# TensorE multiplies a constant in the gaps that its planner leaves

## The chip, the cores and the metric

The kernel runs on one core of a Trainium2 chip. The metric is the device time of one execution in microseconds, as a median of several runs. "PE" is TensorE (the matrix engine), "PEld" its loading of weights, "DVE" VectorE, "ACT" ScalarE, "POOL" GpSimd, "SP" SyncE, which here only issues DMAs. Each engine works through its own instructions strictly in the order in which they were written; engines wait for each other by semaphores.

## The reference: what is computed

One transformer-like block over 2048 tokens of 448 channels: an S4 convolution with adaptive layer norm, then a gated feed-forward layer with another one.

```python
mod = (silu(c) @ w_mod).reshape(6, 448)            # sa, ca, ga, sb, cb, gb
h = layernorm(x) * (1 + ca) + sa
# S4: K[d, l] = Re sum_n C[d,n] * exp(dt*A[d,n] * l) * dt*B[d,n],  448 x 256 complex modes
y = irfft(rfft(pad(h)) * rfft(pad(K))) + h * Dskip
x = x + ga * y
h = layernorm(x) * (1 + cb) + sb
x = x + gb * ((gelu(h @ w_gate) * (h @ w_up)) @ w_down)   # 448 -> 1792 -> 448
```

## The kernel before, in words

The program is written as some 2000 small tasks. Each names the engine (or the choice of engines), a cost in microseconds, a due value, the tasks that it depends on and the buffers that it takes (`Plan.add`, from L148). `Plan.order` (L195) places them one by one: it asks which engine can start soonest, takes for it the ready task with the lowest due value, adds the cost to that engine's clock and sets `t.on` and `t.start`. The due values are corrected by a table of found numbers (`LEAD`, L39). `Plan.run` (L258) then calls each task's function in that order, and the function writes its instructions; so the order of every engine's instructions is the planner's, while the real waits are those of the semaphores that the tile framework adds: an instruction waits for the data that it reads, and the first write to a tile waits until the readers of the buffer before it are done.

The work has three stages.

*Generating the convolution kernel and transforming it (0 to about 375 us).* `prep` (L425) makes the exponents from A, B, C and dt on VectorE and ScalarE and writes them to DRAM as bf16 pieces (`lh_d`), from which `load_lt` fetches them as matmul operands `lt`. `exps` (L583) and `angles` (L621) form exponents and angles on TensorE in PSUM (pool `gen`, two buffers named `pg`), ScalarE takes exp and sin of them, VectorE multiplies (`tx`, `ty`), and `kgen` (L695) sums over the modes with 64 small f32 matmuls into a PSUM tile of the pool `kgp` (buffers `kg`); `ktail` (L720) does a first transform. Meanwhile `mod_row` (L758) makes the rows of `mod`: one DMA of 784 KB (`m.ld`), four f32 matmuls of 448 columns with one column of `c` repeated as weights (`m.mm`, L768), and a copy by ScalarE (`m.ev`, L771). Three rows are needed at the very start; the three DMAs stand on SP's queue behind two 896 KB loads of `x`. `u_norm_a` (L814) normalises `x` and makes the first transform of it (`ua`, L832, two f32 matmuls of 448 columns with 64 rows each), `u_stage_b` and `k_fft` (L959) go on. `m.mm`, `ua` and the transforms share the PSUM pool `fft`, two buffers named `pf`.

*The last part of the transforms and the change-over (about 375 to 425 us).* `t_fft` (L1055) does the last 128 channels; its results go through DRAM into the tile `yi`. `conv_out` (L1227) then makes, for each of the four token groups j of a block, the last transform (`co.mm`, L1246 for the first 320 channels and L1251 for the last 128; for the first block and j below 2 these are two tasks, `co.mme` and `co.mml`, into one PSUM buffer of the pool `pd`), adds `x`, takes the statistics (`co.add`), normalises (`co.n`, L1288 and L1289), transposes the result by an f32 matmul with the identity (`co.t`, L1294 and L1296, into the pool `ps`, six buffers named `pq`) and copies it as f16 high and low parts. This is so for block 0; for the later blocks the transposition is another, in f16 (L1317).

*The feed-forward layer (about 421 us to the end).* `gate_up` (L1338) multiplies with the weights in three f16 products (L1371, L1365), ScalarE takes gelu, VectorE multiplies, and `down_first` and `down` (L1441, L1472) multiply back.

`eps` (L370, L371) is one column of the tile `small`, set to 1e-5 by VectorE as its first instruction; the square roots read it.

## Time and profile before

| | us |
|---|---|
| median of three runs | 823.77 |
| lowest, highest | 823.62, 831.2 |
| the profiled execution, its own time | 825.18 |
| the profiled execution, span from the first to the last instruction | 823.4 |
| TensorE busy in the span | 748.4 |
| VectorE busy | 599.6 |
| ScalarE busy | 470.3 |
| mean granted clock of TensorE | 0.969 |

The profile is of one execution. Its times are counted from the first instruction. A row of the timeline gives the start, the length, the engine, the source line, the operation with the tile that it writes and the one that it reads, a count where neighbouring instructions were merged, and in brackets how long the engine had stood idle before it and what ended that. A row of the waits gives who waited for what, the total in us, how many times, and the longest. A row of a table by stretches gives the busy time of each engine in the stretch (in the order PE, PEld, DVE, ACT, POOL), then the mean granted clock of TensorE (1.00 is full, 0.50 half), the share of the DMA engines' time and the GB/s. The granted clock comes from recorded steps; where none has been recorded yet, the table shows 1.00. Matmul ends are modelled, so that records of matmuls can overlap.

### The profile page before, as it was taken

What the parts mean: (1) busy time and instruction counts of PE and PEld (TensorE: products, weight loads), DVE (VectorE), ACT (ScalarE), POOL (GpSimd) and SP (SyncE); (2) the same over time, 40 slices, a digit from 0 to 9 for tenths busy, and PEclk for the clock granted to TensorE, in tenths of its full rate; (3) what the DMA queues carried; (4) which work ended last, traced back from release to release, by engine and by line L of the source; (5) the groups of instructions that cost most, each with busy time, mean ns of one, the idle gap of its engine ahead of it and who ended that gap; (6) DMA issues with size and microseconds to landing.
All of it is one profiled execution on the core that took longest, in us unless ns stands there. A gap on an engine that the chain in (4) does not pass through costs nothing.

```text
span 823.4 us, 19059 instructions
## 1 busy us (share of the span) xinstructions
PE 748.4 (91%) x8166; PEld 461.2 (56%) x8166; DVE 599.6 (73%) x981; ACT 470.3 (57%) x629; POOL 6.0 (1%) x14
## 2 busy tenths in 40 slices
PE   2786789999799999998589999999999999999997
PEld 1344344444577767778466445444496445864477
DVE  7789998999889989897494783178863686244542
ACT  5598999899968999971244553034442353113320
POOL 0000000000000000000200000000000000000000
PEclk9888799999999999999889999999999999999999
DMA  9552369996858846899669756245315322022101
GB/s 283 148 167 92 105 189 236 285 273 200 236 146 257 233 133 193 253 307 295 189 197 298 267 179 179 75 140 166 117 53 146 135 91 90 34 79 90 45 12 35
DMA packets 92526, 136.83 MB, mean 166 GB/s; under 512 B 21280, under 2 KB 75200, under 8 KB 92442
## 3 DMA queue, kind: packets, MB, share of 16 engines
q1 hardware_dynamic: 89514, 133.75, 53.8%
q10 hardware_dynamic: 2608, 1.61, 0.8%
q8 instruction: 64, 1.05, 0.5%
q0 software_dynamic: 320, 0.26, 0.1%
q14 instruction: 20, 0.16, 0.1%
HBM read 100.48 MB, written 36.01 MB: 166 GB/s over the span
## 4 chain that ended last, share of the span: by engine, by line
PE 67%; ACT 12%; DVE 10%; DMA 6%; issue 3%; SPq 1%; DVEq 0%; ACTq 0%
PE pq L1371 30%; PE pq L1472 9%; PE pd L1441 3%; PE kg L710 3%; ACT fg L643 2%; PE pg L630 2%; PE pf L999 2%; PE pq L1365 2%; PE pf L768 2%; ACT my L617 2%; PE pf L1085 2%; PE pf L895 2%; DVE tx L679 2%; DMA fg<-in_w_mod 2%; PE pd L1472 1%
## 5 line engine op out<-in xcount | busy, mean ns | idle before, releaser
L1371 PE MATMUL pq<-ht,wr 128*128 128x512 f16 (+1 forms) x1200 | 250.0, 367 | 0.0
L1371 PEld LDWEIGHTS <-wr 128*128 128x128 f16 x1200 | 115.4, 98 | 128.6 <-issue 11.0
L1378 ACT ACTIVATE ge<-pq 128x512 f32<-128x512 f32 (+1 forms) x60 | 33.9, 568 | 144.5 <-PE pq L1365 93.9
L1385 DVE TENSOR_TENSOR fq<-ge,pq 128x512 f32<-128x512 f32 (+1 forms) x60 | 38.5, 649 | 72.1 <-PE pq L1371 48.2
L1397 ACT ACTIVATE hh<-fq 128x1024 f16<-128x1024 f32 (+1 forms) x49 | 47.1, 963 | 54.5 <-DVE fq L1385 41.8
L1472 PE MATMUL pq<-d,hh 128*128 128x224 f16 x504 | 73.2, 259 | 0.0
L710 PE MATMUL kg<-ty,tx 128*32 128x64 f32 x3584 | 61.8, 221 | 11.3 <-DVE ty L687 6.4
L679 DVE TENSOR_TENSOR tx<-mx,fg 128x1024 f32<-128x1024 f32 x56 | 68.0, 1220 | 4.0 <-ACT fg L654 2.2
L683 DVE TENSOR_TENSOR ty<-my,fg 128x1024 f32<-128x1024 f32 x56 | 68.2, 1219 | 3.0 <-PE kg L710 2.8
L710 PEld LDWEIGHTS kg<-ty,tx 128*32 128x32 f32 x3584 | 53.0, 110 | 27.6 <-issue 11.2
L1472 PE MATMUL pq<-d,hlo 128*128 128x224 f16 x252 | 65.3, 259 | 0.0
L1400 DVE TENSOR_TENSOR hlo<-fq,hh 128x1024 f16<-128x1024 f32 (+1 forms) x49 | 53.9, 1104 | 5.3 <-ACT hh L1397 5.0
L643 ACT ACTIVATE fg<-pg 128x1024 f32<-128x1024 f32 x56 | 56.6, 1019 | 1.9 <-issue 1.2
L1472 PEld LDWEIGHTS <-hh 128*128 128x128 f16 x588 | 56.7, 98 | 1.1 <-issue 0.4
L617 ACT ACTIVATE my<-pg 128x1024 f32<-128x1024 f32 x56 | 55.3, 1041 | 3.1 <-PE pg L612 2.9
L999 PE MATMUL pf<-q,fc 128*128 128x160 f32 x264 | 42.9, 313 | 0.3 <-DVE q L989 0.3
L630 PEld LDWEIGHTS <-lt 64*128 64x128 bf16 x336 | 20.7, 95 | 37.4 <-issue 20.7
L999 PEld LDWEIGHTS pf<-q,fc 128*128 128x128 f32 x264 | 37.7, 195 | 6.3 <-issue 3.3
L630 PE MATMUL pg<-ea,lt 64*128 64x512 bf16 x168 | 34.9, 389 | 6.2 <-ACT fg L643 4.4
L687 DVE TENSOR_TENSOR ty<-my,fg 128x512 f32<-128x512 f32 x56 | 38.4, 686 | 0.0
L686 DVE SCALAR_TENSOR_TENSOR ty<-my,fg 128x512 f32<-128x512 f32 x56 | 38.4, 685 | 0.0
L735 PE MATMUL kg<-ak,ke 128*64 128x128 f32 x448 | 32.1, 284 | 6.2 <-DVE ke L730 4.4
(172 smaller groups left out, 1196.3 us busy)
## 6 DMA issues: line engine op xcount, KB each, us to landing
wr<-w_d SPq DMA_DIRECT2D x21, 896.0 KB
fc<-in_k_fc SPq DMA_DIRECT2D x20, 576.0 KB
u_d<-so SPq DMA_DIRECT2D x32, 224.0 KB
w<-in_wgu SPq DMA_DIRECT2D x14, 512.0 KB
ui<-u_d SPq DMA_DIRECT2D x10, 672.0 KB
w_d<-wr SPq DMA_DIRECT2D x7, 896.0 KB
fq<-in_wd SPq DMA_DIRECT2D x14, 448.0 KB
us<-uo SPq DMA_DIRECT2D x22, 240.0 KB
```

Source lines behind the costliest of these rows:

```text
L617: A.activation(yb.tile.rearrange("p a b c -> p (a b c)"), pb.tile, AF.Exp)
L630: T.matmul(pa[:, nh * 512:nh * 512 + 512], w, x, start=(k == 0), stop=(k == 2))
L643: A.activation(fb.tile[:, 0].rearrange("p x (n k) -> p n x k", n=2), pb.tile.rearrange("p (n x k) -> p n x k", n=2, x=2), AF.Sin, scale=TW ...
L679: V.tensor_mul(tx.tile, xb.tile[:, xm, None, :].to_broadcast([128, 2, 512]), fb.tile[:, :, 0])
L683: V.tensor_mul(ty.tile[:, 1], yb.tile, fy()[:, 1, :, None, :].to_broadcast([128, 16, 2, 32]))
L710: T.matmul(kg[32 * g:32 * g + 32, 2 * (s % 2) + q, :64], tx[:, r, nh, 4 * q + g], ty[:, r, nh, 4 * q + g], start=(r == 0 and nh == 0), sto ...
L999: T.matmul(pz.tile[:, e % 32 - sl0], fc.tile[:, i, 1 + t], pp.tile[:, t, i], start=(t == 0 and e != 32), stop=(t == 1 and e != 0))
L1371: T.matmul(pb[k].tile[:, ts], wr.tile[:, 4 * lo + t, k, c0:c0 + 128], ht[:, m, ts], start=f % 2 == 0 and i == 0, stop=f % 2 == 1 and i == 9)
L1385: V.tensor_mul(to if half is None else to[:, half:half + 1], *src)
L1397: A.activation(hg.tile[0][:, cb, c], fq.tile[:, c], AF.Copy)
L1400: V.tensor_sub(hg.tile[1][:, cb, c], fq.tile[:, c], hg.tile[0][:, cb, c])
L1472: T.matmul(bank(k)[:, m], x[:, p, q[0], ts], w[:, p, q[1]], start=new and m == 0 and p == 0 and z == 0, skip_group_check=True, stop=i in ( ...
```

## The change

`Plan.run` now notes, for every task that was placed on TensorE, how long the planner's TensorE stands empty in front of it (`t.idle`). A new function `spin` writes matmuls of the constant `eps` with itself into the PSUM tile that the task is about to fill: int((idle - 1.5) / (0.78 w / 448)) of them, w being the columns, if that is positive. The constant is read with stride 0 both as weights (128 x 128) and as the moving operand (128 x w), in f32; each product starts and ends its own accumulation, and the task's own first matmul overwrites the tile. The products are written in front of the task's own matmuls in six kinds of task: `x.mm`, `kgen` (only where it takes a new PSUM tile), `m.mm`, `ua`, `co.mm` with its parts, and `co.t`. The tasks' costs, due values, dependencies and order stay as they are; the planner doesn't count the products.

```diff
     def run(self):
+        free = 0.0
         for t in self.order():
+            if t.on == "PE":
+                t.idle, free = t.start - free, t.start + t.eng["PE"]
             t.fn(t.on) if len(t.eng) > 1 else t.fn()
...
+    def spin(me, dst, w=D):
+        for _ in range(int(max(0.0, me[0].idle - 1.5) / (0.78 * w / D))):
+            T.matmul(dst, eps.to_broadcast([128, 128]), eps.to_broadcast([128, w]), start=True, stop=True)
...
+        me = []
+
         def mm():
             pb.tile = fft.tile([128, D], FT, name="pf")
+            spin(me, pb.tile)
             for t in range(4):
                 T.matmul(pb.tile, c_sb[:, t:t + 1].to_broadcast([DT, 128]), wb.tile[:, t], start=(t == 0), stop=(t == 3))
         t1 = add("m.ld", {"SP": 0.42}, v, ldw, deps[2:], [wb], kb=803)
         t2 = add("m.mm", {"PE": 3.22}, v, mm, [t1, t_si], [pb], [wb])
+        me.append(t2)
...
                 for h in range(2):
                     pbs[h].tile = fft.tile([128, D], FT, name="pf")
+                spin(me, pbs[0].tile)
                 for h in range(2):
                     T.matmul(pbs[h].tile, au[64 * h:64 * h + 64], XT[jb].tile[64 * h:64 * h + 64, j],
                              start=True, stop=True)
             tm = add("ua", {"PE": 0.97}, vv, mm, [tn, c_au], pbs, [XT[jb]])
+            me.append(tm)
...
                     if i == 0:
                         pb.tile = POOLS["pd"].tile([128, D], FT, name="pd")
+                    spin(me, pb.tile[:, c0:c1], c1 - c0)
...
                 pt.tile = POOLS["ps"].tile([128, 4, 128], FT, name="pq")
+                spin(me, pt.tile.rearrange("p k t -> p (k t)")[:, :D])
                 for k in range(3):
                     T.matmul(pt.tile[:, k], xn.tile[:, 128 * k:128 * k + 128], K2["id"], start=True, stop=True)
...
```

In `x.mm` and `kgen` the call is of the same form, on the first 448 columns of the tile `pg` or `kg`.

## The prediction

> **What bounds the kernel now.** I read the page first (busy shares, the 40 slices), then who TensorE waits for, then the stretches where it waits, then the granted clock cut at its own steps. The page:

> ```profile
> span 823.4 us, 19059 instructions
> ...
> PE 748.4 (91%) x8166; PEld 461.2 (56%) x8166; DVE 599.6 (73%) x981; ACT 470.3 (57%) x629; POOL 6.0 (1%) x14
> ...
> PEclk9888799999999999999889999999999999999999
> ```

> TensorE (PE) is busy for 91% of the span, and its clock is below full only in the first fifth and around the middle. Its waits, first up to 424 us, then after:

> ```profile
> PE pf L768 <- DMA fg<-in_w_mod: 16.0, 1, 16.0
> PE pd L1251 <- DMA yi<-y: 10.0, 1, 10.0
> PE pf L832 <- issue: 3.3, 1, 3.3
> PE pq L1294 <- DVE xn L1289: 3.1, 1, 3.1
> ...
> PE pd L1441 <- DVE d L1560: 0.2, 1, 0.2
> ```

> After 424 us TensorE waits 0.2 us in all: there the end is TensorE's work alone, and what is gained before it reaches the end. Before 424 us there are four long single waits, at L768, L832, L1251 and L1294.

> **What is added.** The planner's costs and order don't change; a task's new field `idle` only says how long the planner leaves TensorE empty in front of it. Working the planner's own order() through, the gaps over 1.5 us + one product, at tasks of the six kinds, are four: 14.69 us at the first `m.mm`, 4.16 at the first `ua`, 7.95 at `co.mml` of j=0, 3.67 at `co.t` of j=2. The other gaps over 2.28 us (2.51, 2.38, 2.43) are at `ang`, `anc` and `dn`, which have no product; the longest in front of any `x.mm` or `kgen` is 2.04 us, under 1.5 + 0.78. So the counts are int(13.19/0.78) = 16, int(2.66/0.78) = 3, int(6.45/0.223) = 28 of 128 columns, and int(2.17/0.78) = 2: 49 products, at exactly the four waits above. Nothing else is removed or moved; no DMA is added. Start of the kernel:

> ```profile
> 0.81 0.06 DVE L371 MEMSET small<- 128x1 f32 x1 [0.81 <-PEq L1632]
> ...
> 15.96 12.26 PE L768 MATMUL pf<-fg,pk 112*128 112x448 f32 x24 [15.96 <-DMA fg<-in_w_mod]
> ...
> 20.57 0.34 PEld L768 LDWEIGHTS pf<-fg,pk 112*128 112x128 f32 x1 [0.41 <-issue]
> 21.32 0.34 PEld L768 LDWEIGHTS pf<-fg,pk 112*128 112x128 f32 x1 [0.41 <-issue]
> ...
> 22.24 0.54 ACT L771 ACTIVATE rows<-pf 128x448 f32<-128x448 f32 x1 [6.01 <-PE pf L768]
> ...
> 22.41 0.19 PEld L768 LDWEIGHTS pf<-fg,pk 112*128 112x128 f32 x1 [0.19 <-issue]
> 22.79 0.19 PEld L768 LDWEIGHTS pf<-fg,pk 112*128 112x128 f32 x1 [0.19 <-issue]
> ...
> 24.54 0.42 DVE L544 SCALAR_TENSOR_TENSOR q<-q 112x256 f32<-112x256 f32 x1 [3.78 <-ACT q L540]
> ...
> 28.25 0.54 ACT L771 ACTIVATE gs<-pf 128x448 f32<-128x448 f32 x1 [1.84 <-PE pf L768]
> 28.33 1.38 ACTq L575 DMA_DIRECT2D lt<-lh_d  x2
> ...
> 31.48 1.16 PE L832 MATMUL pf<-xt,au 64*128 64x448 f32 x4 [3.26 <-issue]
> ...
> 33.24 1.39 PE L612 MATMUL pg<-ea,lt 64*128 64x512 bf16 x4 [0.61 <-DMA lt<-lh_d]
> ...
> 36.48 2.39 PE L832 MATMUL pf<-xt,au 64*128 64x448 f32 x4
> ...
> 39.28 1.02 ACT L617 ACTIVATE my<-pg 128x1024 f32<-128x1024 f32 x1 [1.68 <-PE pg L612]
> ```

> One f32 matmul call is two records (24 for the 12 calls of three `m.mm`). They stand 0.75 us apart until 22 us and 0.375 after: a 448-column product costs 1.49 us at half clock and 0.75 at full. (The page shows full clock in the first 22 us because no step is recorded before; the spacing says half.) The granted clock by its own steps, which lie 3.413 us apart:

> ```profile
> 28.83:32.24 3.41, 0.76 (x4) 0.33 (x4) 3.34 (x7) 0.00 (x0) 0.00 (x0) 1.00 1.00 221
> 32.24:35.66 3.42, 2.81 (x11) 1.43 (x10) 2.26 (x4) 2.96 (x4) 0.00 (x0) 0.50 0.33 100
> 35.66:39.07 3.41, 3.41 (x11) 1.62 (x10) 3.19 (x6) 1.83 (x2) 0.00 (x0) 0.50 0.42 69
> 39.07:42.48 3.41, 1.47 (x11) 0.39 (x8) 3.34 (x6) 3.20 (x4) 0.00 (x0) 1.00 1.03 305
> 42.48:45.90 3.42, 2.90 (x17) 1.72 (x14) 3.24 (x9) 3.42 (x6) 0.00 (x0) 0.50 0.36 97
> ...
> 52.72:56.14 3.42, 2.22 (x15) 1.17 (x16) 3.39 (x6) 3.42 (x5) 0.00 (x0) 1.00 0.01 4
> ...
> 83.44:86.86 3.42, 1.85 (x8) 0.79 (x9) 3.35 (x6) 3.39 (x6) 0.00 (x0) 1.00 0.00 0
> 86.86:90.27 3.41, 2.23 (x12) 1.46 (x13) 3.30 (x6) 3.41 (x5) 0.00 (x0) 0.50 0.57 146
> ...
> 370.16:373.57 3.41, 1.54 (x102) 1.38 (x106) 2.82 (x4) 0.60 (x1) 0.00 (x0) 1.00 1.00 372
> ```

> The columns are the stretch, its length, the busy time of PE, PEld, DVE, ACT and POOL, the granted clock, and the DMA engines' share and GB/s. The reader is to see a gate that looks back over one window. After a window with TensorE busy throughout (35.66) the clock is full; after 2.81 us it was not yet. After a full-clock window with 0.76, 1.47 or 1.85 us of work it is half; after 2.22 it stayed, and after the 1.54 of f32 matmuls at 370 too (the page's slices show nothing below nine tenths there). The limit lies somewhere around half a window.

> **A, the 16 products at the start: -3.0 us.** They wait for the memset (0.87) and nothing else; their PSUM bank is fresh. Cutting back by 3.413 from 22.00, a window runs 1.52 to 4.94, so the clock rises at 4.94: (4.94 - 0.95)/1.49 = 2.7 products at half clock, 13.3 x 0.75 = 10.0 us more, end at 14.9, a microsecond ahead of the weights at 15.96. Queued behind them on TensorE is only `m.mm`, which waits for those weights anyway. If the grid lies otherwise, the rise is between 4.4 and 7.8 and the end between 14.6 and 16.3: at worst 0.4 us late. The 24 records then take 24 x 0.375 + 0.2 = 9.2 us instead of 12.26, as no window before holds less than 2.6 us of work. Later weights are no obstacle, as the DMA engines are nearly idle from 21 us and the third set is used at 21.9 (the second at 18.95, estimated from the first at 15.96 and the last by 21 to land near 18.5):

> ```profile
> 21.00:22.00 1.00, 1.00 (x2) 0.34 (x1) 0.00 (x0) 0.00 (x0) 0.00 (x0) 1.00 0.14 53
> ```

> Who gains: ScalarE's (ACT) copy at 22.24, idle 6.01 us for it; through it the arctangent and VectorE's (DVE) L544, idle 3.78; the copy at 28.25; and the load of `lt` right behind that on ACT's DMA queue, for which L612 at 33.24 waits. Each slack is larger than the 3.0 it must give, and 28.25 itself waited for TensorE. Bounds: 0.4 lost to 3.1 won.

> [...]

> **B, three products before `ua`: -1.2 us.** Their bank is free once ACT has read the second `m.mm`, about 22.8 in the new time; they run from 24.9 to 27.2 and `ua` is due at 28.5, so they delay nothing. Without cover they would cost 2.25. The window 25.41 to 28.83 then has 2.1 us of work and the next about 2.4 (`ua` 0.8, L612 0.75, `ua` again), between the 1.85 that lost the clock and full. With full clock where 32.24 to 39.07 was at half, the 2.39 us `ua` takes about half, and the L612 behind it comes in time for ACT, which sat idle 1.68 us. Bounds 0 and -1.7; I take -1.2, because the clock's survival is close, and nearer to the whole because both windows hold about the 2.22 that kept it.

> **C, 28 short products, and D, two before `co.t`.**

> ```profile
> 395.72 3.29 PE L1085 MATMUL pf<-q,my 128*128 128x128 f32 x28
> 398.94 1.30 PE L1246 MATMUL pd<-yi,ai 128*64 128x320 f32 x8
> ...
> 410.23 1.32 PE L1251 MATMUL pd<-yi,ai 128*64 128x128 f32 x8 [9.99 <-DMA yi<-y]
> ...
> 420.25 0.94 PE L1294 MATMUL pq<-ident,xn 128*128 128x128 f32 x6 [3.07 <-DVE xn L1289]
> 421.54 3.92 PE L1371 MATMUL pq<-ht,wr 128*128 128x256 f16 x20
> ...
> 425.72 2.36 PE L1371 MATMUL pq<-ht,wr 128*128 128x256 f16 x20
> ...
> 417.95:421.36 3.41, 1.11 (x10) 0.94 (x10) 3.33 (x8) 3.25 (x6) 0.00 (x0) 1.00 0.00 0
> 421.36:424.77 3.41, 3.41 (x20) 2.29 (x17) 3.34 (x7) 0.89 (x1) 0.00 (x0) 0.50 0.48 154
> ```

> A 128-column product is two records of 3.29/28 us: 0.235. C is 28 x 0.235 = 6.6 us inside a wait of 9.99 (13.2, or 3.2 late, if all ran at half clock; they follow dense work, so they start at full). About 3 us of idling is left behind them, nearly a window, so the clock may fall after all; and from 410 to 420 VectorE is the chain, not TensorE. Bounds 0 and -0.4; taken as 0. D: 2 x 0.75 = 1.5 us inside 3.07 (3.0 at half clock, still inside). Idle in any window is then at most 1.6 us, busy at least 1.8, in f32 products as at 370, where 1.54 kept the clock. So the clock that falls at 421.36 after 1.11 busy should stay, and the first 20 matmuls of L1371 take 2.36 instead of 3.92: -1.6, bounds 0 and -1.7. From 421.54 TensorE is the bound, so it stays to the end.

> **Sum.** -3.0 - 1.2 + 0 - 1.6 = -5.8 us, against the profiled execution's 825.18 us (span 823.4 and 1.8 around it): 819.4. That execution lies 1.4 above the median 823.77; on the median the forecast is 818.0.

> **Rivals.** (1) The shift is won at the start and the clock falls otherwise: work moved by 3 to 4 us lies differently on windows 3.413 long, so B and D can fail. For it: 1.8 to 2.4 us of work is no safe margin beside the 1.85 that failed. Then only A: 820.8. (2) The middle swallows A and B, as VectorE and ScalarE are nearly always busy there (3.34 and 3.20 of 3.41 us at 39.07). Against: they are late, not full, and nothing I saw has a start of its own. Only D: 822.2. (3) The half-clock windows further on are partly spared too; three windows at half clock cost 3 x 3.41/2 = 5.1 us of TensorE work, of which about half would lie on the path: 818.0 - 2.6 = 815.4. (4) The other side: products of a constant occupy TensorE without raising its clock. Then 16 x 1.49 = 23.8 us from 0.95 end at 24.8, `m.mm` starts 8.8 us late and still at half clock, and the rest moves by that: 832.6. It decides as soon as the clock rises after 7.1 us, when (7.1 - 0.95)/1.49 = 4.1 products are done and 11.9 x 0.75 = 8.9 us reach 15.96; each later microsecond costs 0.5. Against: L768 itself, with one column repeated as weights, raised the clock in two windows. That the change does less than it says is certain in one way: it reaches four places, not the half-clock stretches between 42 and 97 us.

> [...]

> **How the numbers follow.** Forecast 0.56, rival 1 0.18, rival 2 0.10, rival 3 0.11, rival 4 0.05. A measurement of this kernel tells about 1% (8.2 us) from no change: faster than 815.5 takes half of rival 3 and the forecast's tail, 0.06 each, so 0.12; slower than 832.0 is rival 4, 0.05; within 0.83. The range reaches from all bounds won (-3.1 - 1.7 - 0.4 - 1.7 = -6.9, 816.9) on past rival 3 to 814.8, and up past rival 2 to 823.2; outside it are rival 4 and some of the tails.

> **What would show it.** Right: 32 product records from about 0.95, spaced 0.75 then 0.375, ended before L768; L768 near 9.2 us long; ACT's first L771 near 19.2 and L612 near 30.2; no ACT wait of 1.7 us near 35; two products after the second `co.t`, and the first 20 of L1371 in about 2.4 us. Wrong: L768 starting after 16.4, half clock during L768 or the first L1371, or an early gain that is gone by 360 us.

## The result and the profile after

| | before | after |
|---|---|---|
| median of 19 runs each, us | 825.46 | 818.65 |
| lowest, highest | 820.12, 831.76 | 815.12, 823.71 |
| after / before, 95% interval | | 0.9902, 0.988 to 0.9923 |
| the profiled execution, its own time | 825.18 | 821.08 |
| its span | 823.4 | 819.3 |
| its mean granted clock | 0.969 | 0.971 |

The ratio is worth 8.1 us of 825.46 (6.4 to 9.9). The forecast was 5.8 less, 818.0. The number came out; most of what made it did not come from the terms of the sum. The page after:

```profile
span 819.3 us, 19253 instructions
...
PE 771.5 (94%) x8264; PEld 476.9 (58%) x8264; DVE 599.0 (73%) x981; ACT 470.5 (57%) x629; POOL 6.0 (1%) x14
...
PEclk9897699999999999998999999999999999999999
```

TensorE is busy 23 us longer and has 98 more matmul records: 49 products of two. The start, TensorE's rows of the timeline:

```profile
0.92 15.35 PE L417 MATMUL pf<-small 128*128 128x448 f32 x32 [0.92 <-DVE small L392]
16.11 9.18 PE L784 MATMUL pf<-fg,pk 112*128 112x448 f32 x24
...
28.52 1.02 PE L852 MATMUL pf<-xt,au 64*128 64x448 f32 x4 [0.96 <-DVE xt L840]
31.01 0.60 PE L623 MATMUL pg<-ea,lt 64*128 64x512 bf16 x1 [1.47 <-DMA lt<-lh_d]
32.07 1.03 PE L623 MATMUL pg<-ea,lt 64*128 64x512 bf16 x3 [0.46 <-DMA lt<-lh_d]
```

(L768 of before is L784 here, L832 is L852, L612 is L623.) The products do what the first term said: `m.mm` takes 9.18 us where it took 12.26. ScalarE behind it:

```profile
19.32 0.54 ACT L788 ACTIVATE rows<-pf 128x448 f32<-128x448 f32 x1 [3.56 <-PE pf L784]
...
25.33 0.54 ACT L788 ACTIVATE gs<-pf 128x448 f32<-128x448 f32 x1 [1.84 <-PE pf L784]
25.41 1.38 ACTq L582 DMA_DIRECT2D lt<-lh_d  x2
...
37.74 2.86 ACT L628 ACTIVATE my<-pg 128x1024 f32<-128x1024 f32 x3 [1.66 <-PE pg L623]
```

Everything is 2.9 us earlier up to the issue of the load of `lt` (25.41 against 28.33). Then half of it is lost: the load's data release the first matmul at 31.01 and the rest at 32.07, where in before all four went from 33.24, and ScalarE's wait, which ends at 37.74, is as long as it was (1.66 us, in before 1.68). The clock in these stretches (columns as in the prediction):

```profile
27.50:30.91 3.41, 1.08 (x5) 0.30 (x4) 3.33 (x6) 1.28 (x2) 0.00 (x0) 1.00 1.05 233
30.91:34.33 3.42, 2.86 (x9) 1.33 (x10) 0.80 (x2) 2.17 (x3) 0.00 (x0) 0.50 0.37 117
```

With `lt` late, the window held 1.08 us of work and the clock fell, as it had in before. Now the middle, which the prediction didn't speak of. TensorE's waits of the kind "issue" (no other engine or DMA explains them), before and then after:

```profile
PE kg L710 <- issue: 3.4, 1, 3.4
PE pf L832 <- issue: 3.3, 1, 3.3
PE kg L735 <- issue: 1.8, 2, 1.5
```

```profile
PE kg L748 <- issue: 0.6, 1, 0.6
PE kg L722 <- issue: 0.3, 1, 0.3
```

The first fence is from the very view that the prediction read; its largest row, 3.4 us in one piece, was passed over there for the row below it, with which the change has to do. Where it stands, in before:

```profile
221.67 1.88 PE L710 MATMUL kg<-ty,tx 128*32 128x64 f32 x107
226.93 0.86 PE L710 MATMUL kg<-ty,tx 128*32 128x64 f32 x21 [3.38 <-issue]
227.71 3.11 PE L999 MATMUL pf<-q,fc 128*128 128x160 f32 x12
```

and the same work in after:

```profile
219.20 1.10 PE L722 MATMUL kg<-ty,tx 128*32 128x64 f32 x64
220.80 0.31 PE L722 MATMUL kg<-ty,tx 128*32 128x64 f32 x5 [0.50 <-DVE ty L698]
221.44 1.08 PE L722 MATMUL kg<-ty,tx 128*32 128x64 f32 x59 [0.34 <-issue]
222.45 1.90 PE L1020 MATMUL pf<-q,fc 128*128 128x160 f32 x12
```

TensorE of before stops in the middle of one `kgen`, after 107 of its 128 records, where the profile shows no engine and no DMA that it waits for. The stop fills a window, and the clock is gone in the next:

```profile
223.38:226.80 3.42, 0.17 (x11) 0.01 (x1) 1.55 (x2) 3.30 (x4) 0.00 (x0) 1.00 0.16 43
226.80:230.21 3.41, 3.29 (x30) 3.12 (x31) 2.32 (x3) 0.38 (x1) 0.00 (x0) 0.50 0.02 5
```

so that L999 takes 3.11 us where it takes 1.90 in after. Stop and clock together are (3.38 - 0.34) + (3.11 - 1.90) = 4.2 us. To see what reaches the path I set the n-th VectorE instruction of the one trace against the n-th of the other: after is 2.9 us early at 25 us, 1.6 at 37, 1.9 at 215, then 6.5 at 245. So 4.6 us, more than any term of the forecast, arise between 215 and 245 us, where the change writes no product.

What TensorE waits for there is, by the traces, its program. The page lists the queue q8 as one of instructions, and the DMA view of before between 224.4 and 225.6 us has one packet of it (16,384 bytes, begun at 224.45 and ended at 225.54 by the packed trace), the only one from 218.2 to 227.9; TensorE goes on 1.4 us after its end. The rows of the page of before and of that stretch (packets, MB, share of the 16 DMA engines):

```profile
q8 instruction: 64, 1.05, 0.5%
```

```profile
q8 instruction: 1, 0.02, 5.7%
```

The trace of before has 2 x 8166 records of matmuls and weight loads and 76 others on TensorE, 16,408 instructions: 64 packets are one for about 256 of them. Counted so, the stop stands after instruction 5313 = 20 x 256 + 193, and the other one of before (1.51 us at 360.8, inside L735) after 10177 = 39 x 256 + 193. In all 14 traces of this study each "issue" wait of TensorE, 30 in all without those at `ua`, stands after a number that is 193 modulo 256; such places are called block ends from here on. The change writes 16 + 3 products ahead of that `kgen`, each of two records and two weight loads: 76 instructions, so the same block ends after 107 - 76/2 = 69 records, and there its 0.34 us stand (64 + 5).

The last two groups of products, in after:

```profile
396.70 6.52 PE L417 MATMUL pd<-small 128*128 128x128 f32 x56
407.75 1.36 PE L1275 MATMUL pd<-yi,ai 128*64 128x128 f32 x8 [4.54 <-DMA yi<-y]
...
415.16 1.77 PE L417 MATMUL pq<-small 128*128 128x448 f32 x4
417.81 0.94 PE L1322 MATMUL pq<-ident,xn 128*128 128x128 f32 x6 [0.88 <-DVE xn L1314]
...
419.05 0.61 PE L1400 MATMUL pq<-ht,wr 128*128 128x256 f16 x4
419.83 1.91 PE L1400 MATMUL pq<-ht,wr 128*128 128x256 f16 x16 [0.18 <-DVE ht L1332]
```

Behind the 28 products TensorE still idles 4.54 us and loses the clock (half from 406.38 to 413.21). The two at `co.t` keep it: 20 records of L1400 in 2.7 us, where L1371 took 3.92; the shift grows by 1.3 from 411 to 437 us.

### The profile page after: what moved, and what is told of

Read it like the earlier page. It is cut to its first block, busy times and chain, and to the rows that moved or that the text cites. A ratio compares the mean times of both kernels' runs of the same rounds, so it can differ in the third digit from the quotient of the medians.

```text
span 819.3 us, 19253 instructions
## 1 busy us (share of the span) xinstructions
PE 771.5 (94%) x8264; PEld 476.9 (58%) x8264; DVE 599.0 (73%) x981; ACT 470.5 (57%) x629; POOL 6.0 (1%) x14
## 4 chain that ended last, share of the span: by engine, by line
PE 72%; ACT 10%; DVE 7%; DMA 6%; issue 3%; SPq 2%; ACTq 0%; DVEq 0%
PE pq L1400 30%; PE pq L1501 9%; PE pg L641 4%; PE pd L1470 4%; PE kg L722 3%; PE pf L916 3%; ACT fg L654 2%; PE pq L1394 2%; DMA q<-us 2%; ACT my L628 2%; PE pf L417 2%; PE pf L852 2%; PE pf L784 2%; PE pf L1106 2%; PE pf L1020 2%
## 5 line engine op out<-in xcount | busy, mean ns | idle before, releaser
L1400 PE MATMUL pq<-ht,wr 128*128 128x512 f16 (+1 forms) x1200 | 248.6, 365 | 0.2 <-DVE ht L1332 0.2
L1400 PEld LDWEIGHTS <-wr 128*128 128x128 f16 x1200 | 114.5, 98 | 128.2 <-issue 11.3
```

The source lines that it names most:

```text
L1400: T.matmul(pb[k].tile[:, ts], wr.tile[:, 4 * lo + t, k, c0:c0 + 128], ht[:, m, ts], start=f % 2 == 0 and i == 0, stop=f % 2 == 1 and i == 9)
```

## The experiments

Theory: the gain is of two parts, the clock kept at full by the products, and block ends of TensorE's program that the products' own instructions shift. Rival: all of it is the clock. Each of the twelve kernels was timed on one chip with the kernel before, in 6 to 12 runs; the chips differ, so kernels are compared by their ratios. "Added" is what a kernel adds to TensorE's instructions ahead of the stop near 222 us; "stops" is the sum of TensorE's "issue" waits without the one at `ua`, from its profile.

| kernel | added | stops, us | median, us | ratio, 95% |
|---|---|---|---|---|
| before | 0 | 5.1 | 825.46 to 828.0 | 1 |
| the change | 76 | 0.9 | 818.65 | 0.9902, 0.988 to 0.9923 |
| e1 start alone | 64 | 2.1 | 822.28 | 0.9927, 0.9899 to 0.9956 |
| e2 `co.mml` alone | 0 | 6.1 | 827.83 | 0.9999, 0.9974 to 1.0023 |
| e3 `co.t` alone | 0 | 5.0 | 828.02 | 0.9995, 0.9971 to 1.0019 |
| e4 start and `co.t` | 64 | 1.9 | 819.5 | 0.9913, 0.988 to 0.9945 |
| e5 padding alone | 64 | 2.0 | 821.47 | 0.9938, 0.9912 to 0.9963 |
| e6 start, padded to a block | 256 | 6.5 | 827.2 | 1.0003, 0.9967 to 1.004 |
| e7 more products | 88 | 4.5 | 820.55 | 0.9932, 0.99 to 0.9964 |
| e8 the change, padded to a block | 256 | 4.8 | 824.52 | 0.996, 0.9929 to 0.9992 |
| e9 the change and 52 | 128 | 0.0 | 819.27 | 0.991, 0.9878 to 0.9942 |
| e10 the change and 116 | 192 | 1.6 | 819.85 | 0.9919, 0.9889 to 0.9948 |
| e11 e9 with `lt` covered | 128 | 0.3 | 818.37 | 0.99, 0.9858 to 0.9941 |
| e12 padding alone | 128 | 0.0 | 821.71 | 0.9928, 0.9898 to 0.9957 |

### One part alone: e1, e2, e3, e4

```diff
     def spin(me, dst, w=D):
+        if me[0].n not in ("m.mm",):
+            return
```

with `("co.mml",)`, `("co.t",)` and `("m.mm", "co.t",)` in e2, e3 and e4.

> Only the 16 products in front of the first m.mm. Theory (the sum of the prediction): L768's matmuls run at full clock, 9.2 us instead of 12.3, everything after moves by 3.0 us: ratio to before about 0.9964, 822.5 where before is 825.5. Rival (given back): the load of lt still lands late, half of the 3.0 is lost by 40 us: ratio 0.998. Rival (luck of the clock's grid): later half-clock stretches fall otherwise and the ratio can be anything from 0.992 to 1.0 with no tie to the 3.0.

> Only the 28 short products in front of co.mml. Theory: about 3 to 4.5 us of idling are left behind them, the clock still falls before or just after the last transform, and VectorE is the chain there: ratio 1.000, within 0.0005. Rival (the warm stretch counts): the clock is full from 410 to 420 and the ratio is 0.997 or lower.

> Only the two products in front of the transposition of j=2. Theory: the first 20 matmuls of L1371 run at full clock, 2.4 us instead of 3.9: ratio 0.998. Rival (the clock is still at half there without the 28 products before): no change, ratio 1.000, and the first 20 still take 3.9 us.

> The 16 at the start and the two in front of the transposition. Theory: -3.0 and -1.6 add up: ratio 0.9944, and the whole change (0.9902) is better by no more than the three products in front of ua bring. Rival (the 28 short products matter): ratio 0.996 to 0.997, clearly above the whole change.

The products at the start carry the most, 0.9927, which is 6.0 us of 827.69 and twice the 3.0 forecast for them. e1's trace gives the reason away: it is 2.9 us early at 215 us and 8.1 at 245, with no stop in that `kgen`. e2 is worth nothing, as C said. e3 alone shows nothing either (its interval is 2 us to each side), though in its trace as in e4's the shift grows by 1.3 us across `co.t`. From start alone to start and `co.t` the ratio falls by 0.0014, 1.2 us, inside the intervals. e4's 0.9913 is below the 0.9944 expected, as e1's is below its 0.9964: both have the 64 instructions.

### Padding without products: e5 and e12

```diff
+    def tiny(dst, n):
+        for i in range(n):
+            g = 32 * (i % 4)
+            T.matmul(dst[g:g + 32, :1], eps.to_broadcast([128, 32]), eps, start=True, stop=True, tile_position=(0, g))
+
     def spin(me, dst, w=D):
-        for _ in range(int(max(0.0, me[0].idle - 1.5) / (0.78 * w / D))):
-            T.matmul(dst, eps.to_broadcast([128, 128]), eps.to_broadcast([128, w]), start=True, stop=True)
+        if me[0].n == "m.mm" and me[0].idle > 10:
+            tiny(dst, 16)
```

One such product of one column is four instructions too. e12 has `tiny(dst, 32)`.

> In place of the 16 products at the start stand 16 products of one column (32 x 1), so TensorE's program is as much longer (64 instructions) but the clock should not rise before the first m.mm; no other products. The profile of before shows TensorE stopping for 3.4 us at 223.6 with nothing named, in the midst of one kgen, and a 16 KB fetch of instructions starting only at 224.5; none of the runs with the 16 products shows that stop, all without do. Theory P (place): what counts is where in the program the 256-instruction blocks end; then the stop is gone here too and the ratio is 0.993 to 0.996, with L768 still 12 us long. Theory T (time): the stop is avoided because the work comes 2 to 3 us earlier on the DMA engines' backlog; then it stays, ratio 1.000.

> None of the change's products: 32 one-column products (128 instructions, about a microsecond of TensorE) in front of the first m.mm alone. They don't keep TensorE busy long enough to raise the clock, so the first m.mm takes its 11 to 12.3 us as before. Theory of block ends: the long stops of before near 222 and 360 us are gone, as in the runs with 128 instructions more, and with them 3.5 to 5.5 us: ratio 0.993 to 0.996. Rival (the gain needs the products, and padding by 64 was chance): within 0.998 to 1.002.

e12, its start, the `kgen` that stopped in before, and TensorE's one "issue" wait, that at `ua`:

```profile
0.92 1.03 PE L418 MATMUL pf<-small 128*32 128x1 f32 x64 [0.92 <-DVE small L392]
15.13 11.65 PE L789 MATMUL pf<-fg,pk 112*128 112x448 f32 x24 [13.17 <-DMA fg<-in_w_mod]
...
223.33 1.10 PE L727 MATMUL kg<-ty,tx 128*32 128x64 f32 x64 [0.49 <-DVE ty L703]
224.40 1.90 PE L1025 MATMUL pf<-q,fc 128*128 128x160 f32 x12
```

```profile
PE pf L857 <- issue: 3.3, 1, 3.3
```

`m.mm` takes 11.65 us, so the clock was not raised ahead of it; no block end stops TensorE any more; and the kernel is 6.0 us faster (0.9928). Set against before, its trace is 0.6 us late at 215 us and 4.5 early at 245. e5, with 64 instructions, is as theory P said: `m.mm` takes 10.91 us, the `kgen` near 222 us doesn't stop, and the ratio is 0.9938. A microsecond of TensorE's time, which doesn't raise the clock, gives three quarters of what the whole change gives. The rival, that all of the gain is the clock, is refuted.

### The products with the block ends put back: e6 and e8

e6 writes `tiny(dst, 54)` and 10 products at the first `m.mm`, 256 instructions, and nothing elsewhere. e8 is the whole change, with

```diff
-        for _ in range(int(max(0.0, me[0].idle - 1.5) / (0.78 * w / D))):
+        n = int(max(0.0, me[0].idle - 1.5) / (0.78 * w / D))
+        if n == 16:
+            tiny(dst, 46)
+            n = 15
+        for _ in range(n):
```

> 54 products of one column and 10 of 448 at the start, 256 instructions in all, so that the blocks of 256 end where they did before; the clock rises and m.mm runs at full clock if they end by 16 us. Theory P: the stop of 3.4 us is back at the same instruction of the same kgen (after 107 of its 128 records), and the ratio is 0.997 to 0.998, the half-clock gain alone. Theory T: no stop, ratio 0.993 as with the 16 products.

> The whole change, with 15 products of 448 columns in place of 16 at the start and 46 one-column products (32 weights, f32, 4 instructions each) ahead of them: 184 + 60 + 12 (the three at ua) = 256 instructions more on TensorE than before, by the middle of the program, where the change has 76. Theory (the stops of TensorE stand at the ends of blocks of 256 of its own instructions, and the change's extra gain was that 76 instructions shifted these ends): the start is as in the change (the f32 m.mm in 9.2 to 9.6 us), but the block ends stand again where they stood before, so the stop of 3.0 to 3.8 us comes back after 107 of the 128 records of the kgen near 222 us, and the clock falls behind it; the time is 3.5 to 5.5 us above the change's, a ratio of 0.995 to 0.998. Rival (the stop is a matter of what else moves at that time, and the shift of the whole by 2 us at the start removed it): no stop there, ratio 0.990 as the change.

e6 and then e8:

```profile
16.31 10.92 PE L791 MATMUL pf<-fg,pk 112*128 112x448 f32 x24 [4.27 <-DMA fg<-in_w_mod]
...
228.90 0.86 PE L729 MATMUL kg<-ty,tx 128*32 128x64 f32 x21 [3.78 <-issue]
```

```profile
15.56 9.26 PE L793 MATMUL pf<-fg,pk 112*128 112x448 f32 x24
...
30.30 0.60 PE L632 MATMUL pg<-ea,lt 64*128 64x512 bf16 x3 [1.03 <-DMA lt<-lh_d]
...
222.48 0.53 PE L731 MATMUL kg<-ty,tx 128*32 128x64 f32 x21 [3.26 <-issue]
```

With a whole block more, the stop is back at the same record, the 108th (21 are left), and so is the second one of before (now after instruction 10177 + 256). e6, whose products end 4.27 us too early and lose the clock again, gains nothing. e8 keeps the clock gain and loses 0.0058 against the change, 4.8 us. Since e8's profiled execution kept the clock after its stop, its span was 815.8 us; its 12 runs have the median 824.52.

### Other block ends: e9 and e10

e9 is the change with `tiny(dst, 13)` ahead of the 16, e10 with `tiny(dst, 29)`.

> The whole change with 13 one-column products (52 instructions) ahead of the 16: 128 instructions more than before instead of 76. Theory of block ends: in the kgen where the stop of before stood the block now ends after 107 - 64 = 43 of 128 records; any stop over 0.3 us in the whole run without another engine as its cause stands at an instruction whose number is 193 modulo 256, counted as before. How long each stop is isn't foretold by the theory; the time is the change's within 4 us, ratio 0.986 to 0.995. Rival (stops belong to places in the work, not to block ends): a stop, if any, after 69 or 107 records as in the change or before.

> The whole change with 29 one-column products (116 instructions) ahead of the 16: 192 instructions more than before instead of 76. Theory of block ends: in the kgen where the stop of before stood the block now ends after 107 - 96 = 11 of 128 records, and stops elsewhere move alike, all at numbers 193 modulo 256; the time is the change's within 4 us, ratio 0.986 to 0.995. Rival: stops at the same places in the work as in the change.

In e10 the `kgen` runs through, and the next end, 256 instructions on, falls 11 records into the group behind it:

```profile
221.43 1.76 PE L1028 MATMUL pf<-q,fc 128*128 128x160 f32 x11
224.79 0.30 PE L1028 MATMUL pf<-q,fc 128*128 128x160 f32 x1 [1.60 <-issue]
```

In e9 no block end stops TensorE for long. How long a stop is can be read from the packets. The n-th packet of q8 begins, as a rule, within 5 us of the n-th block end; here it stands beside the end that comes next (times of the packed traces, in us):

| kernel, block end after | end before it | packet | TensorE goes on | from end to end without the stop | stop |
|---|---|---|---|---|---|
| before, 5313 | 219.63 | 224.45 to 225.54 | 226.92 | 3.92 | 3.38 |
| before, 10177 | 357.25 | 359.71 to 360.86 | 362.34 | 3.57 | 1.51 |
| e8, 5569 | 215.19 | 219.78 to 220.99 | 222.48 | 4.03 | 3.26 |
| the change, 5313 | 214.42 | 218.67 to 219.80 | 221.44 | 6.68 | 0.34 |
| e12, 5313 | 216.50 | 218.13 to 219.41 | 222.33 | 5.83 | none |

All 30 stops end 1.28 to 1.64 us after the end of that packet, and none of the 889 block ends of the 14 traces (without the first of each) was passed sooner than 1.22 us after it. By these times a stop is what is left when TensorE does the work between two ends faster than the packet comes; an edit moves the ends to other work, 3.92 us of it in before and 5.83 in e12. What makes a packet late was not tested. It goes with the load of the DMA engines: over the 2 us behind a block end their share of time is 0.98 on average where the packet began 2 to 3 us after the end, and 0.56 where it began 0 to 1 us after it.

### Covering the late load: e7 and e11

e7 is the change with 44 products at `co.mml` and three in front of the first `y.mm`; e11 is e9 with `tiny(dst, 10)` and these three:

```diff
                     pb.tile = gen.tile([128, 1024], FT, name="pg")
+                    if once:
+                        once.pop()
+                        for _ in range(3):
+                            T.matmul(pb.tile[:, :D], eps.to_broadcast([128, 128]), eps.to_broadcast([128, D]), start=True, stop=True)
```

> The whole change with 3 more products in front of the first y.mm (where TensorE waits for lt) and 44 in place of 28 in front of co.mml. Theory: the clock stays full from 27 to 38 us and from 404 to 425; ACT's wait of 1.7 us near 36 us is gone and the start keeps its whole 3.0: 1.5 us less than the whole change, ratio 0.988. Rival: what is filled there is off the chain, ratio 0.990 as the whole change; or the 16 added records move the blocks of instructions and a stop appears elsewhere: 0.994.

> The whole change, with 10 one-column products ahead of the 16 and 3 products of 448 columns in front of the first y.mm (which waits for lt): 64 + 12 + 12 + 40 = 128 instructions more than before by the middle, block ends as in the run with 52 instructions more than the change. Theory of B (the clock fell there because TensorE idled for lt, 1.08 us of work in that window): the three products fill the wait, the clock stays full from its first rise to past 36 us, ScalarE's wait of 1.66 us for the y.mm shrinks to about 0.6; worth 1.0 to 1.7 us at 37 us, and if nothing further back takes it, a ratio 0.001 to 0.002 below that run's 0.991. Rival (the middle swallows it): the wait shrinks as said, but the shift is back at 2 us by 50 us and the ratio is 0.991.

e7, and e11 with ScalarE's row:

```profile
220.35 1.09 PE L729 MATMUL kg<-ty,tx 128*32 128x64 f32 x63
223.02 1.11 PE L729 MATMUL kg<-ty,tx 128*32 128x64 f32 x65 [1.57 <-issue]
```

```profile
29.33 2.53 PE L635 MATMUL pg<-small 128*128 128x448 f32 x6
31.80 0.60 PE L637 MATMUL pg<-ea,lt 64*128 64x512 bf16 x4
...
35.67 3.77 ACT L642 ACTIVATE my<-pg 128x1024 f32<-128x1024 f32 x4 [0.58 <-PE pg L637]
```

In both the clock is still full at 39 us (four records of 256 columns take 0.40 us at 39.15 in e7 and 0.39 at 39.49 in e11; in e8, at half clock, 0.61 at 37.78), and ScalarE's wait falls from 1.66 to 0.58. At 37 us e11 is 2.6 us early, where the change is 1.6. But e7 adds 12 more instructions, its block ends after 63 records, and there TensorE stops 1.57 us; other stops come to 3.0. It has the most products and, at 0.9932, less gain than the change. e11, with quiet ends, has 0.99, lower than e9's 0.991 by no more than the measurement leaves open. No kernel here is told apart from the change as faster.

## Why the prediction was right, and where it was wrong

**The total** came out (818.0 forecast, 818.65 measured; 5.8 against 6.8 between the medians, 8.1 by the ratio), but as a sum of other terms, and that is luck: too much was expected of the clock, and nothing of the block ends.

**A, 16 products, -3.0.** Right up to the load of `lt`: the clock rose at 7.02, within the 4.4 to 7.8, `m.mm` took 9.18 (9.2), ScalarE's first copy came at 19.32 (19.2). Rival 4 fell with the same row: the constant products raised the clock. The step that failed is "Each slack is larger than the 3.0 it must give": of 2.9 us only 1.2 got through the load (32.07 against 33.24): it needed 6.7 us from its issue to the last data (25.41 to 32.07), in before 4.9 (28.33 to 33.24). The DMA engines' share is 1.05 in that stretch; whether their load made it slow was not tested.

**B, -1.2.** Nothing came in the profiled change: the window that should hold `ua` and L612 had 1.08 us of work, since L612 was late, and A's failure is B's. Where `lt` came a little sooner the reckoning held. e8's windows:

```profile
26.30:29.73 3.43, 2.02 (x8) 0.46 (x6) 3.36 (x6) 0.58 (x2) 0.00 (x0) 1.00 0.86 205
29.73:33.14 3.41, 2.43 (x13) 1.44 (x15) 3.04 (x6) 3.40 (x4) 0.00 (x0) 1.00 0.60 204
33.14:36.56 3.42, 1.93 (x11) 0.38 (x7) 3.31 (x7) 3.30 (x4) 0.00 (x0) 1.00 1.01 257
```

2.02 and 2.43 us of work kept the clock, 1.93 didn't (it was half from 36.56 on), and e8 is 4.3 us early at 37 us: A and B as forecast together, -4.2. In this case B hangs on when `lt` comes and on where the windows lie.

**C, 0.** Right: the clock fell behind it all the same (half from 406.38 in after), and e2 is at 0.9999. e7's 44 products kept it (eight records of L1282 in 0.85 us, where L1275 takes 1.36 in after), and nothing was won: e7 is 5.1 us early at 395 us and 5.2 at 411. The products end at 405.26, when the last traced transfer to `yi` has just landed (405.10); the chain behind that is mostly VectorE's.

**D, -1.6.** Right in mechanism, 1.3 in the traces of the change, e3 and e4.

**What the sum left out** is larger than any of its terms: the block ends, 4.8 us (e8 against the change) to 6.0 (e12 against before). With the ends held fixed, all the products are worth 1.5 us at 128 instructions (e9 against e12) and 3.3 at a whole block (e8 against before, 0.7 to 5.9), where 5.8 were forecast; the start alone is worth 0.9 at 64 instructions (e1 against e5), where 3.0 were. Each has an uncertainty of 2 us and more, so that the first and the last can't be told from nothing. By these figures a quarter to six tenths of the forecast came from the clock, and a gain that no one planned made up the rest. The prediction took TensorE's waits for "exactly the four" that the change fills, and did not ask of the 3.4 us at L710, in the same view, what an added instruction does to it.

**The rivals.** The first was half right (B fell, D held), the second wrong (1.9 us are still there at 215 us), the third fits some executions, of which only the mean clock is on record. After's 19 executions show mean clocks of 0.969 to 0.983; the three at 0.982 and more took 815.1 to 815.6 us, the four up to 0.971 took 821.1 to 823.7. The profiled one, at 821.08, is one of these: it lost the clock once more at 368.83 (half until 375.66), after this window, and its end is only 4.0 us early:

```profile
365.37:368.80 3.43, 1.50 (x72) 1.34 (x74) 1.75 (x5) 0.00 (x0) 0.00 (x0) 1.00 1.05 380
```

## What to carry to other kernels

The instructions that were added on TensorE moved the block ends of its later program (76 of them from behind 107 records of a `kgen` to behind 69, 88 to behind 63; on the other engines nothing was measured); so read the "issue" waits inside groups of matmuls first, and time a padding of the same number of instructions as a control before crediting an edit with its effect. Where a program has such stops, some cheap instructions at an idle place are a lever of their own (here 128 for 6.0 us), to be tried at several counts: here the stop went where the block end moved to a place with more work between two ends (5.83 us in e12, 3.92 in before). Ask what the work behind a warmed clock waits for: here a load that was next in the chain took 1.7 of the 2.9 us back (32.07 against 33.24), while the 1.3 us in front of the feed-forward layer, where TensorE alone sets the pace, stayed (after is 3.7 us early at 437 us and 4.0 at 800).
